# Sixteen subtractions of weight halves on VectorE instead of GpSimd, and the conversion steps grouped at the head of a pair's step

## The chip, the cores and the metric

One core of a Trainium2 chip runs the whole kernel. The metric is the device time of one execution in microseconds (us); lower is better. Times are medians over several runs.

## The reference

Two parts follow each other. The attention part takes `q`, `k`, `v` of 4 batches, 8 heads, 576 positions and 64 features. It computes causal softmax attention, and mixes it head by head with a linear memory read-out:

```
scores = causal(q @ k.T / 8);  a = softmax(scores);  local = a @ v
q_p = elu(q) + 1
mem_out = (q_p @ M_prev) / (q_p . z_prev + 1e-6)
x = sigmoid(beta) * mem_out + (1 - sigmoid(beta)) * local
```

The second part takes the 2304 rows of `x`, each of 512 features, through four weight matrices that are given in float64 and used as float32:

```
out = ((x @ w1) * (x @ w2)) @ w3 @ w_out      # 512->1024, 1024->1024, 1024->512
```

## The kernel before

**Pairs.** The attention runs over 16 pairs of heads, four to a batch (`pair_step(p, F)`). A pair's work is cut into named pieces: transposes of the softmax rows (`t1`, `t2`, `th`, `t3a` and so on, line 236), the memory path of the next pair (`ma`, `mb`, `mc`, lines 138 to 159), the transposes of its result (`mt`, line 165), the products with `v` and `M_prev` (`mm`, `pv`, lines 273 to 283), the copy of the result into two parts `xs` (`fin`, lines 294 and 295: ScalarE writes the high part, VectorE the low part and with that frees the PSUM tile `x`), then the next pair's scores (`ss`, line 205 into `s` and into `sx`, which uses the PSUM space that `fin` frees), their masked row minima (`s_red`, line 182 on VectorE), exponentials (`e0` to `e4`, line 217 on ScalarE) and normalisation (`n2` to `n4`, lines 221 to 226 on VectorE).

**Filler.** The string `ORDER` lists the pieces of one pair. At every `F` the TensorE gets some matmuls of another job: during the first batch `w_gen`, which forms the product `w3 @ w_out` (line 429, then `wH` on ScalarE, line 434, and `wL` on VectorE, line 421); from the second batch on `moe_gen`, the two products of the rows that the batch before gave (lines 479 and 499). There are 13 such slots to a pair.

**Conversion.** Weights arrive as float64, read as pairs of 32-bit words. `conv_stages` turns a piece of 128 x 512 into float32 in stages: a load (line 305), `scale` on ScalarE (line 316, output `wp`, `w3s` or `wo`), `join` with two VectorE instructions (lines 320 and 321), and for the first products' weights (pieces 24 to 39) a `split`: ScalarE rounds `wp` into the high part in `wsp` (line 328), GpSimd subtracts it and writes the low part (line 329). A piece's buffer `wp` comes free for another `scale` once line 329 has run. The letter `c` in `ORDER` is one step of this pipeline (two from the second batch on): it splits piece k-2, joins piece k-1, asks for loads up to k+1 and scales piece k. `tick_ok` refuses a step while the product `w3 @ w_out` is not far enough (pieces 12 to 23), and refuses pieces from 32 on during the first batch; a filler that needs a piece asks for it itself with `conv_upto`.

**Who sets the order.** The program order gives priorities. A list scheduler lays out each engine's queue when the program is built: an engine takes the highest priority among what is ready by the scheduler's own clock, and `tc.high_priority` raises a few instructions. On the chip each queue then runs in that fixed order, and an instruction that waits holds all that stand behind it on its engine.

Of the kernel before, what the change touches and what calls it, by code (L numbers as in the profile page):

```python
# [13 lines left out]
ALU = mybir.AluOpType  # L14
# [4 lines left out]


ORDER = (
    "lv mt t1 c F "
    "lqn t2 th c F "
    "t3a t3b c F "
    "t4a c F "
    "t4b t5 c F "
    "mm pv ma c F "
    "fin F "
    "ss lq mb F "
    "F "  # L30
# [7 lines left out]
def f32(ap):  # L38
    return ap.bitcast(F32)
# [3 lines left out]
def attention_moe_kernel(  # L43
# [13 lines left out]
    nc = tc.nc  # L57
# [240 lines left out]
    def conv_stages(k, src, dh, dl):  # L298
        n = 512
        box = {}  # L300

        def load():
            t = x_p.tile([128, 2 * S], F32, tag=f"x{4 + k % 3}", name="wst")
            box["raw"] = t[:, 0:2 * n].bitcast(U32).rearrange("p (n w) -> p n w", w=2)
            nc.sync.dma_start(out=t[:, 0:2 * n].bitcast(U32), in_=src.bitcast(U32))

        def scale():
            if k < 24:
                box["raw"] = raws[src[0]][:, src[1]]
            if k < 24:  # L310
                box["p"] = dh()
            elif k < 36 and k % 4 > 1:
                box["p"] = big.tile([128, n], F32, tag=f"r{4 + k % 4}", name="wp")
            else:
                box["p"] = o_p.tile([128, n], F32, tag="o", name="wp")
            nc.scalar.activation(out=box["p"], in_=f32(box["raw"][:, :, 1]), func=ACTF.Prelu, scale=2.0 ** -111, alpha=-(2.0 ** 32))

        def join():
            p = box["p"].bitcast(U32)
            nc.vector.tensor_scalar(out=p, in0=p, scalar1=3, scalar2=None, op0=ALU.logical_shift_left)  # L320
            nc.vector.scalar_tensor_tensor(  # L321
                out=p, in0=box["raw"][:, :, 0], scalar=29, in1=p, op0=ALU.logical_shift_right, op1=ALU.bitwise_or
            )

        def split():
            if k < 24:
                return
            nc.scalar.activation(out=dh(), in_=box["p"], func=ACTF.Copy)
            nc.gpsimd.tensor_tensor(out=dl(), in0=box["p"], in1=f32(dh()), op=ALU.subtract)  # L329

        return load, scale, join, split

# [84 lines left out]
    def w_gen():  # L417
        box = {}

        def low(i):  # L420
            nc.vector.scalar_tensor_tensor(  # L421
                out=wL[i], in0=box.pop(i), scalar=2.0 ** -16, in1=f32(wH[i]), op0=ALU.mult, op1=ALU.subtract
            )

        def mm(ps, i, kc):
            conv_upto(max(wo_job[kc], w3_job[i][kc // 4]))
            w = big_t["w3", i]
            wo = big_t["wo", kc // 2]
            nc.tensor.matmul(ps, lhsT=w[:, 128 * kc:128 * kc + 128], rhs=wo[:, 512 * (kc % 2):512 * (kc % 2) + 512], start=(kc == 0), stop=(kc == 7))  # L429

        def high(i, ps):
            w_done[0] += 1
            with tc.high_priority(100):
                nc.scalar.activation(out=wH[i], in_=ps, func=ACTF.Copy, scale=2.0 ** -16)
            box[i] = ps

        first = [ps_m.tile([128, DM], F32, tag="m", name="m") for _ in range(2)]
        for kc in range(8):
            for i in range(2):
                mm(first[i], i, kc)  # L440
                if kc == 7:
                    high(i, first[i])
                yield 870
        low(0)
        for i in range(2, NF):
            ps = ps_m.tile([128, DM], F32, tag="m", name="m")
            for kc in range(8):
                mm(ps, i, kc)
                yield 870
                if kc == 0:  # L450
                    low(i - 1)
            high(i, ps)
        low(NF - 1)
# [55 lines left out]
    def moe_gen(b):  # L509
        for n in (2 * b, 2 * b + 1):  # L510
            yield from gemm1(n)
            while 128 * (done_g[0] + 1) <= U * (n + 1):
                yield from gemm2(done_g[0])
                done_g[0] += 1
# [34 lines left out]
    def pair_step(p, F):  # L549
# [46 lines left out]
        out=mask[:, 448:576], in_=mask[:, 448:576], pattern=[[-1, 128]], compare_op=ALU.is_ge,  # L596
# [14 lines left out]
    F = Fill(w_gen(), W_NS, SLOTS * NC + PRE, wait=-4)  # L611
# [38 lines left out]
    for b in range(B):  # L650
        load_m(b)
        if b:
            limit[0] = NJ + 2
            F = Fill(moe_gen(b - 1), MOE_NS, SLOTS * NC)
# [3 lines left out]
    F = Fill(moe_gen(B - 1), MOE_NS, 1)  # L658
# [34 lines left out]
```

## Time and profile before

| | us |
|---|---|
| median of 3 runs | 572.43 (571.6 to 573.46) |
| the profiled execution, its own time | 571.37 |
| its span, first to last instruction | 569.6 |
| outside the span (571.37 - 569.6) | 1.77 |

The span is the time between the first and the last instruction of the profiled execution, which runs 1.77 us longer than its span and 1.06 us shorter than the median. Busy time is the time in which an engine had an instruction in execution, waits not counted.

### The profile page before, as it was taken

The numbers are of one execution on the slowest core, as the hardware profiler recorded it, in microseconds if no ns is written. First come the engines' busy times: TensorE is split into PE (matmuls) and PEld (weight loads), VectorE is DVE, ScalarE is ACT, GpSimd is POOL, SyncE is SP. The second block draws the span as 40 slices with busy tenths as digits, with TensorE's granted clock in tenths as the row PEclk, the third lists the DMA queues.
The fourth block names the chain that finished last, engine by engine and source line by source line (L and its number), as shares of the span: only waits on it lengthen the run. The fifth ranks groups of instructions, "written<-read, shape, count | busy, mean of one in ns | idle before, by whom it ended". The sixth has DMA issues, their size and how long they took to land.

```text
span 569.6 us, 9266 instructions
## 1 busy us (share of the span) xinstructions
PE 545.4 (96%) x3440; PEld 436.4 (77%) x3440; DVE 279.4 (49%) x880; ACT 277.5 (49%) x723; POOL 126.6 (22%) x153
## 2 busy tenths in 40 slices
PE   4899897899999999999999999999999999999997
PEld 2344554456797889788988898797969797998995
DVE  6986797838662626263726272724535351111111
ACT  5565785648562546454644455444635362130210
POOL 1101333015613032303230313021310320130220
PEclk9899989799999999999999999999999999999999
DMA  7991653713021312130202121322012000001001
GB/s 292 421 379 49 223 181 121 223 48 102 31 68 29 105 29 67 34 109 29 66 20 92 29 68 34 91 64 68 26 36 99 23 1 6 33 1 38 1 1 55
DMA packets 23069, 48.31 MB, mean 85 GB/s; under 512 B 6896, under 2 KB 13040, under 8 KB 21488
## 3 DMA queue, kind: packets, MB, share of 16 engines
q1 hardware_dynamic: 23024, 47.72, 25.1%
q8 instruction: 27, 0.44, 0.3%
q14 instruction: 18, 0.15, 0.1%
HBM read 43.00 MB, written 4.72 MB: 84 GB/s over the span
## 4 chain that ended last, share of the span: by engine, by line
PE 82%; DVE 8%; ACT 4%; issue 2%; POOL 2%; DMA 2%; SPq 0%; POOLq 0%; DVEq 0%
PE m L479 36%; PE m L499 18%; PE x L283 7%; PE s L236 7%; PE s L205 4%; PE m L429 4%; PE x L274 2%; PE sx L205 2%; DVE sm L226 2%; PE x L165 1%; DVE sm L182 1%; POOL wsp L329 1%; DMA wst<-w_out 1%; ACT pt L267 1%; PE s L191 1%
## 5 line engine op out<-in xcount | busy, mean ns | idle before, releaser
L479 PE MATMUL m<-xs,wsp 128*128 128x288 f32 x1536 | 221.6, 299 | 1.3 <-DVE wL L421 1.3
L479 PEld LDWEIGHTS m<-xs,wsp 128*128 128x128 f32 x1536 | 206.7, 188 | 2.3 <-DVE wL L421 1.5
L491 POOL TENSOR_TENSOR ht<-a,ht 128x288 fp32r<-128x288 f32 (+2 forms) x96 | 57.6, 612 | 237.5 <-ACT ht L490 237.5
L217 ACT ACTIVATE sm<-sm,mx 128x320 f32<-128x320 f32 (+2 forms) x144 | 82.7, 576 | 39.5 <-DVE mx L182 38.5
L499 PE MATMUL m<-wH,ht 128*128 128x512 f32 x288 | 94.2, 396 | 0.0
L488 DVE SCALAR_TENSOR_TENSOR a<-m,a 128x288 f32<-128x288 f32 x64 | 29.1, 455 | 99.1 <-PE m L479 94.7
L267 ACT ACTIVATE pt<-s 128x512 f32<-128x512 f32 (+1 forms) x144 | 63.3, 492 | 25.1 <-PE s L236 25.0
L429 PE MATMUL m<-wo,w3s 128*128 128x512 f32 x128 | 65.5, 647 | 6.2 <-DVE w3s L321 3.8
L499 PEld LDWEIGHTS m<-wH,ht 128*128 128x128 f32 x288 | 54.1, 188 | 11.2
L490 ACT ACTIVATE ht<-a 128x288 fp32r<-128x288 f32 (+2 forms) x96 | 31.5, 360 | 63.2 <-DVE a L488 63.1
L236 PE MATMUL s<-ident,sm 128*128 128x128 f32 x448 | 61.7, 273 | 0.0
L236 PEld LDWEIGHTS s<-ident,sm 128*128 128x128 f32 x448 | 52.7, 140 | 7.2 <-issue 5.8
L226 DVE TENSOR_SCALAR sm<-sm,sums 128x320 f32<-128x320 f32 (+2 forms) x144 | 57.1, 457 | 0.4
L182 DVE CUSTOM_DVE_ANT_0 sm<-s,mask 128x320 f32<-128x320 f32 (+3 forms) x112 | 44.4, 448 | 24.4 <-PE s L205 24.3
L499 PE MATMUL m<-wL,ht 128*128 128x512 f32 x144 | 56.2, 390 | 0.0
L146 POOL TENSOR_TENSOR e<-qn,z 128x640 f32<-128x640 f32 x16 | 25.3, 1581 | 136.3 <-DVE qn L144 112.9
L485 ACT ACTIVATE a<-m 128x288 f32<-128x288 f32 x64 | 26.1, 408 | 50.7 <-PE m L479 45.4
L429 PEld LDWEIGHTS m<-wo,w3s 128*128 128x128 f32 x128 | 24.4, 209 | 31.3 <-issue 20.0
L283 PEld LDWEIGHTS x<-pt,v 128*64 128x64 f32 x384 | 25.1, 137 | 29.9 <-issue 24.0
L283 PE MATMUL x<-pt,v 128*64 128x448 f32 (+4 forms) x384 | 46.7, 393 | 0.0
L295 DVE TENSOR_TENSOR xs<-x,xs 128x576 fp32r<-128x576 f32 x16 | 12.1, 756 | 66.6 <-ACT xs L294 66.6
L205 PE MATMUL s<-raw 64*128 64x320 f32 (+3 forms) x256 | 38.3, 414 | 4.5 <-DMA raw<-qkt 4.5
(65 smaller groups left out, 474.3 us busy)
## 6 DMA issues: line engine op xcount, KB each, us to landing
raw<-qkt SPq DMA_DIRECT2D x16, 576.0 KB, 3.9
wst<-w3t SPq DMA_DIRECT2D x8, 1024.0 KB, 8.9
wst<-w SPq DMA_DIRECT2D x16, 512.0 KB, 3.8
qn<-qn SPq DMA_DIRECT2D x16, 320.0 KB, 3.0
v<-v SPq DMA_DIRECT2D x32, 160.0 KB, 2.3
out<-o SPq DMA_DIRECT2D x18, 256.0 KB, 2.0
wst<-w_out SPq DMA_DIRECT2D x4, 1024.0 KB, 12.0
z<-z_prev SPq DMA_DIRECT2D x16, 64.0 KB, 2.9
```

The source lines that it names most:

```text
L182: nc.vector.tensor_tensor_reduce(out=sm[a][c][:, lo:hi] if c else sm0[:, 0:64], in0=x, in1=mask[:, S - KE[c] + lo:S - KE[c] + hi] if c els ...
L205: nc.tensor.matmul(y, lhsT=t[r, 0, 128 * c - 64:128 * c + 64], rhs=t[r, 1, lo:hi], start=True, stop=True)
L217: nc.scalar.activation(out=x, in_=x, func=ACTF.Exp, bias=mx, scale=-1.0, accum_out=sums_of(p)[:, k:k + 1])
L226: nc.vector.tensor_scalar(out=x, in0=x, scalar1=sums_of(p)[:, k:k + 1], scalar2=None, op0=ALU.mult)
L236: tr = lambda o, c, a, kc: nc.tensor.transpose(ps[:, o:o + 128], sm[a][c][:, 128 * kc:128 * kc + 128], ident)
L267: nc.scalar.activation(out=d, in_=s, func=ACTF.Copy)
L283: nc.tensor.matmul(x[64 * a:64 * a + 64, 384 + q0:384 + q1], lhsT=vv[:, a, kc], rhs=pt[:, a, o:o + q1 - q0], start=False, stop=(q0 == 0 or ...
L429: nc.tensor.matmul(ps, lhsT=w[:, 128 * kc:128 * kc + 128], rhs=wo[:, 512 * (kc % 2):512 * (kc % 2) + 512], start=(kc == 0), stop=(kc == 7))
L479: nc.tensor.matmul(ps[:, 0:U], lhsT=w[:, i, x, j], rhs=x_t[NC * b + j][:, xx, U * u:U * u + U], start=(k == 0), stop=(k == 11))
L490: nc.scalar.activation(out=hbuf(f, 0)[:, p:p + c], in_=a[:, o:o + c], func=ACTF.Copy)
L491: nc.gpsimd.tensor_tensor(out=hbuf(f, 1)[:, p:p + c], in0=a[:, o:o + c], in1=f32(hbuf(f, 0)[:, p:p + c]), op=ALU.subtract)
L499: nc.tensor.matmul(ps, lhsT=hbuf(f, a)[:, p:p + 128], rhs=b[f], start=(k == 0), stop=(k == 23))
```

## The change

Two edits. The subtraction at the end of `split` is issued on VectorE where it was issued on GpSimd: sixteen instructions of 128 x 512, with the same operands. And in `ORDER` the six letters `c`, which stood one each before the first six slots of a pair, stand two, two, one and one before its first four slots.

```
 ORDER = (
-    "lv mt t1 c F "
-    "lqn t2 th c F "
+    "lv mt t1 c c F "
+    "lqn t2 th c c F "
     "t3a t3b c F "
     "t4a c F "
-    "t4b t5 c F "
-    "mm pv ma c F "
+    "t4b t5 F "
+    "mm pv ma F "
     "fin F "
...
             nc.scalar.activation(out=dh(), in_=box["p"], func=ACTF.Copy)
-            nc.gpsimd.tensor_tensor(out=dl(), in0=box["p"], in1=f32(dh()), op=ALU.subtract)
+            nc.vector.tensor_tensor(out=dl(), in0=box["p"], in1=f32(dh()), op=ALU.subtract)
```

## Rows read from the trace of the kernel before

**Rows 1.** The page: busy us of each engine, share of the span, instructions.

```profile
PE 545.4 (96%) x3440; PEld 436.4 (77%) x3440; DVE 279.4 (49%) x880; ACT 277.5 (49%) x723; POOL 126.6 (22%) x153
```

**Rows 2.** Busy time by stretch: length, engines, PE clock, DMA; pairs 1 to 3, the rest.

```profile
60.00:81.10 21.10, 18.70 (x98) 11.14 (x99) 18.15 (x60) 17.34 (x43) 8.54 (x8) 0.92 0.62 200
81.10:110.90 29.80, 24.98 (x111) 13.52 (x110) 25.37 (x58) 18.65 (x43) 7.81 (x6) 0.89 0.51 163
110.90:133.10 22.20, 22.20 (x112) 12.47 (x111) 13.25 (x49) 13.45 (x35) 4.25 (x4) 1.00 0.31 90
...
162.00:569.60 407.60, 403.93 (x2749) 351.87 (x2747) 152.90 (x514) 172.73 (x472) 81.94 (x112) 1.00 0.14 45
```

**Rows 3.** The instructions of line 329 by stretch: length, POOL busy (count), PE clock, DMA.

```profile
60.00:81.10 21.10, 5.68 (x5) 0.92 0.62 200
110.90:133.10 22.20, 1.45 (x2) 1.00 0.31 90
60.00:150.00 90.00, 22.25 (x16) 0.94 0.42 133
```

**Rows 4.** Waits of PE from 60 to 150 us: total us, times, longest.

```profile
PE sx L205 <- DVE xs L295: 5.5, 2, 3.2
PE s L191 <- DVE mx L182: 1.6, 1, 1.6
PE m L479 <- DVE wL L421: 1.3, 1, 1.3
```

**Rows 5.** Timeline of PE: start, us, instruction.

```profile
73.58 7.68 PE L429 MATMUL m<-wo,w3s 128*128 128x512 f32 x14
...
104.21 6.86 PE L429 MATMUL m<-wo,w3s 128*128 128x512 f32 x12
...
127.88 5.37 PE L429 MATMUL m<-wo,w3s 128*128 128x512 f32 x12
```

**Rows 6.** Timeline of DVE in pair 2: start, us, instruction, idle before it.

```profile
88.93 1.68 DVE L320 TENSOR_SCALAR wp<-wp 128x512 uint32<-128x512 uint32 x1 [0.22 <-ACT wp L316]
...
97.53 1.04 DVE L320 TENSOR_SCALAR wp<-wp 128x512 uint32<-128x512 uint32 x1 [1.25 <-ACT wp L316]
...
99.21 0.75 DVE L295 TENSOR_TENSOR xs<-x,xs 128x576 fp32r<-128x576 f32 x1
...
100.33 1.63 DVE L321 SCALAR_TENSOR_TENSOR wp<-wst,wp 128x512 uint32<-128x512 uint32 x1
```

**Rows 7.** Timeline of POOL in the same stretch.

```profile
88.79 1.54 POOL L146 TENSOR_TENSOR e<-qn,z 128x640 f32<-128x640 f32 x1 [6.60 <-DVE qn L144]
...
97.02 1.26 POOL L329 TENSOR_TENSOR wsp<-wp,wsp 128x512 fp32r<-128x512 f32 x1 [1.75 <-ACT wsp L328]
100.04 1.38 POOL L329 TENSOR_TENSOR wsp<-wp,wsp 128x512 fp32r<-128x512 f32 x1 [1.75 <-ACT wsp L328]
```

**Rows 8.** Groups of instructions, whole run: count, busy us, mean ns, idle before.

```profile
L329 POOL TENSOR_TENSOR wsp<-wp,wsp 128x512 fp32r<-128x512 f32 x16 | 22.3, 1395 | 29.6 <-ACT wsp L328 29.5
...
L321 DVE SCALAR_TENSOR_TENSOR wp<-wst,wp 128x512 uint32<-128x512 uint32 x16 | 14.3, 892 | 0.4
...
L320 DVE TENSOR_SCALAR wp<-wp 128x512 uint32<-128x512 uint32 x16 | 10.3, 641 | 5.1 <-ACT wp L316 5.1
...
L328 ACT ACTIVATE wsp<-wp 128x512 fp32r<-128x512 f32 x16 | 10.1, 637 | 7.6 <-DVE wp L321 7.6
...
L320 DVE TENSOR_SCALAR w3s<-w3s 128x512 uint32<-128x512 uint32 x16 | 6.7, 420 | 1.6 <-ACT w3s L316 1.5
...
L421 DVE SCALAR_TENSOR_TENSOR wL<-m,wH 128x512 fp32r<-128x512 f32 x8 | 5.5, 683 | 3.2 <-ACT wH L434 3.2
```

**Rows 9.** Waits of ACT from 60 to 150 us.

```profile
ACT wp L316 <- POOL wsp L329: 3.8, 4, 1.5
```

**Rows 10.** Timeline of DVE, the normalisations of two successive pairs.

```profile
110.36 2.02 DVE L226 TENSOR_SCALAR sm<-sm,sums 128x320 f32<-128x320 f32 x7
...
130.84 4.09 DVE L226 TENSOR_SCALAR sm<-sm,sums 128x320 f32<-128x320 f32 x7
```

## Prediction

> **What bounds the kernel now.** I first read the page's busy line: TensorE (PE) is busy 545.4 of 569.6 us, 96% [rows 1]. Then I cut the span by pairs, each stretch beginning where PE takes up the five transposes of line 165. From 162 us to the end PE is busy 403.93 of 407.60 us at full granted clock [rows 2]; no conversion runs there, so the change has nothing to move. All sixteen of its subtractions lie between 60 and 150 us [rows 3]. In that part pair 3 is the nearly clean case: 22.20 us, PE busy throughout, granted clock 1.00, and 1.45 us of line 329 at its very end [rows 2, 3]. Pair 2 does the same PE work (111 records against 112) in 29.80 us, 7.60 longer, at a mean clock of 0.89 [rows 2]. So the question is what holds PE in pairs 1 and 2 and at the start of the second batch.
>
> The third view, PE's waits, names three places [rows 4]: `sx` waits for `fin`'s low part (line 295, VectorE, called DVE) 5.5 us in two waits, the score of block 0 waits for the row minima (line 182, DVE) 1.6 us, and the first batch product waits for `wL` (line 421, DVE) 1.3 us. All three releasers are DVE. A slow clock comes on top: twelve matmuls of line 429 take 5.37 us at clock 1.00 and 6.86 us behind the waits of pair 2; fourteen take 7.68 us behind the wait of pair 1 (5.5 - 3.2 = 2.3 us) [rows 4, 5], where 14/12 of 5.37 would be 6.27. The slow clock thus costs about 1.5 us in pair 2 and 1.4 in pair 1.
>
> The last view says why DVE is late: the timelines of DVE and GpSimd (POOL) side by side. Line 320 takes 0.420 us on `w3s` (mean of 16), but 1.68 us when it starts 0.14 us behind a POOL instruction of 1.54 us, and 1.04 us inside POOL's line 329; line 321 takes 1.63 us beside another line 329 and ends 0.54 us after it [rows 6 to 8]. In these rows a DVE instruction that meets a POOL one runs only when that has ended.
>
> **What the change removes.** Sixteen instructions leave POOL, 22.3 us in all, 1.395 each [rows 8]. POOL is busy for 126.6 us of the span, so its own time is worth nothing; what counts is whom it holds. The conversion's DVE instructions show that by group: line 320 averages 0.641 us on `wp` against 0.420 on `w3s`, line 321 averages 0.892 against 0.683 for line 421, the nearest unhindered form of that size [rows 8]. That is 16 x 0.221 + 16 x 0.209 = 6.9 us, part of it owed to POOL's other lines 146 and 159, which stay. Seven normalisations take 4.09 us at 130.84 against 2.02 one pair before: 2.1 more [rows 10]. Also ScalarE (ACT) waits 3.8 us in four waits for line 329 to free `wp` [rows 9].
>
> **What it adds.** Sixteen DVE subtractions of 128 x 512. None is in the trace; the nearest row, line 421, has the same size and takes 0.683 us. So 16 x 0.683 = 10.9 us of DVE work, against some 9.0 us of hindrance (6.9 + 2.1), of which lines 146 and 159 keep a part. DVE's total hardly falls. The gain, if any, is in position: the release of `wp` comes 1.395 - 0.683 = 0.7 us sooner per piece, and instructions on the path are no longer held.
>
> One page speaks against the edit: the Trainium skill, "SBUF — State Buffer", section "Who interferes with whom", says that a DVE instruction with two SBUF inputs contends with a GpSimd instruction that reads SBUF, and that the second to start fully blocks. The trace agrees where it can: line 321 has two such inputs and took 1.63 us beside POOL's 1.38 [rows 6, 7]. By it the moved subtraction can itself be held by lines 146 and 159, each time by up to 1.54 us; if four of the sixteen met them in full, the gain below of 3.1 us would shrink to nothing.
>
> **Pair 2.** The chain in front of `sx` is: line 320 at 97.53 (held 1.04 - 0.42 = 0.62 us), line 321, line 295 at 99.21; behind it line 321 at 100.33 (held 1.63 - 0.68 = 0.95 us), in front of the row minima [rows 6]. Taking line 329 off POOL removes 1.57 us there. Two pieces release 0.7 us earlier each: 1.4. Two subtractions now stand in DVE's queue at these places: +1.4 (2 x 0.683). Net -1.6 us of waiting, of 4.8 in this pair (3.2 + 1.6). A third of the 1.5 us of slow clock should go with it: -0.5. I take -1.9, rounding down. Ends: the whole excess over pair 3, -7.6, and +1.4 if the subtractions come in front and nothing else moves.
>
> **Pair 1.** Its 2.3 us wait is also for line 295. Which instruction holds DVE there the rows above do not say, and POOL also runs lines 146 and 159 in this pair. I take 0. Ends: -3.7 (the wait and its 1.4 us of slow clock) and +0.7 (one subtraction in front of line 295).
>
> **Start of the second batch.** Line 421 stands behind the normalisations that lost 2.1 us; PE waits 1.3 us for it [rows 4, 10]. Line 421 is older in program order than the subtractions beside it, so these should fall behind it. I take -1.2. The other end is 0, where two subtractions (1.4 us) go ahead.
>
> **The moved steps.** From the code's counts: in pair 0 pieces 16 and 17 are now refused, since the filler has not ended its first product by slots 3 and 4, and go to pair 1; pieces 18 to 31 stay in their pairs, earlier by up to two slots; pieces 36 to 39 move from slots 3 and 4 of pair 4 to slot 2. Each step takes its load, `scale`, `join` and `split` along, and the loads pass that of `qn` on the DMA queue, which is asked for a whole pair ahead of its transposes. I cost this at nothing. The pieces do not run at their place now: five of the subtractions already run in pair 1 [rows 3], though their steps belong to pair 2 and later. Readiness of a load and of a `wp` buffer decides, and priority only settles ties. If that cover is gone, the price is one `scale` and one `split` of ACT ahead of a `pt` copy: about 1.3 us (2 x 0.637) in pair 4.
>
> **Sum.** -1.9 + 0 - 1.2 + 0 = -3.1 us. Against the profiled execution's own 571.37: 568.3. That execution was 1.06 us under the median of the runs, so the median becomes 569.3, 0.55% less.
>
> **Rivals.** (a) *Clean pair.* Without POOL's holds, `fin` and the minima come in time, and pair 2 runs like pair 3: -7.6, with -1.3 for the batch start: 571.37 - 8.9 + 1.06 = 563.5. For it: pair 3 shows that the PE work fits 22.2 us. Against: DVE is busy 25.37 us in pair 2 [rows 2], which holds the hindrance but would also hold the new work.
>
> (b) *The lock only changes sides.* The subtraction is held by lines 146 and 159, or stands where the hindrance stood; 10.9 us in, 9.0 out. No change: 571 to 573.5. For it: the two totals are near, and lines 146 and 159 remain.
>
> (c) *DVE's queue waits for ACT.* This is the slower side. On POOL a subtraction waited 29.6 us in total for line 328 and held nothing that mattered [rows 8]. On DVE it holds all behind it. If each of some eight subtractions between 60 and 110 us arrives one line 328 (0.637 us) early, DVE stands 5.1 us, on top of 8 x 0.683 = 5.5 of work; about half of the 9.0 us of hindrance goes, 4.5. That is +6.1 us on DVE in two pairs where it releases every PE wait; with -1.2 at the batch start +4.9: 577.3. It decides once 3 of the eight are held with DVE followed by PE: 3 x 0.637 + 5.5 - 4.5 - 1.2 = +1.7 us. For it: ACT already waits 7.6 us for DVE in front of line 328 [rows 8], so queue orders and real times disagree there. Against: DVE has idle time in these pairs too (2.95 and 4.43 us).
>
> **Numbers.** Forecast 0.45 (of it 0.03 within 0.3%), (a) 0.12, (b) 0.20, (c) 0.23. Within 0.3% (1.7 us) is what a measurement of this kernel cannot tell from no change. Faster 0.42 + 0.12 = 0.54; same 0.23; slower 0.23. The range goes from (a), 563.5, to just below the far end of (c), which needs all eight held: 576.5. The forecast's own range is 566.5 to 571.5.
>
> **What would show it.** Right: no DVE instruction beside a missing line 329 is held; line 320 on `wp` falls towards 0.42 us mean; subtractions at 0.68 us; the waits of `sx` for line 295 fall from 5.5 to about 4; the wait for line 421 is gone; nothing changes behind 162 us but the start. Wrong: DVE idle in front of line 329 with line 328 as the releaser, pair 2 still near 29.8 us, a clock below 0.9 in pairs 1 or 2, or a new PE wait in pair 4 for `pt`. The queue order is laid out anew, so a piece that lands ahead of line 295 can move the sum by the size of a whole wait.

## The result and the profile after

The changed kernel takes 567.19 us (median of 4 runs, 566.53 to 568.34) against 572.5 for the kernel before (4 runs): a ratio of 0.9909 with a 95% interval of 0.9886 to 0.9933, 0.9% faster. A second series gave 568.14 us, ratio 0.9926 [0.9908, 0.9945]. The forecast was 569.3, 0.55% faster. The profiled execution took 566.9 us, 4.5 less than the one before, with a span of 565.1.

The page's busy line, to set against [rows 1]. POOL has 16 instructions and 20.5 us less; DVE has 16 instructions more and yet 1.2 us less busy time.

```profile
PE 544.0 (96%) x3440; PEld 435.1 (77%) x3440; DVE 278.2 (49%) x896; ACT 277.0 (49%) x723; POOL 106.1 (19%) x137
```

Busy time by stretch, cut where PE takes up line 165, as in [rows 2]: pairs 1, 2 and 3. Both tables begin at 60.00, a little after pair 1 does.

```profile
60.00:79.10 19.10, 16.93 (x97) 9.88 (x96) 16.18 (x50) 15.48 (x39) 3.27 (x2) 1.00 0.61 202
79.10:107.30 28.20, 24.43 (x112) 12.91 (x111) 24.86 (x73) 20.53 (x49) 3.21 (x2) 0.94 0.52 171
107.30:129.50 22.20, 22.20 (x112) 12.47 (x111) 13.81 (x50) 13.58 (x35) 2.80 (x2) 1.00 0.36 115
```

The waits of PE from 60 to 150 us, to set against [rows 4]. The wait of `sx` is nearly halved, that for line 421 is gone, that for the row minima has grown, and a new one of 0.5 us for line 226 stands in pair 2.

```profile
PE sx L205 <- DVE xs L295: 2.9, 2, 1.9
PE s L191 <- DVE mx L182: 2.3, 1, 2.3
PE s L236 <- DVE sm L226: 0.5, 1, 0.5
PE s L236 <- ACT pt L267: 0.3, 1, 0.3
```

PE's queue holds the same instructions in the same order in both kernels, so the two timelines can be laid on each other. Pair 1 begins at 59.62 (60.08 before), pair 2 at 79.08 (81.10), pair 3 at 107.30 (110.91), pair 4 at 129.46 (133.08); the products with `M_prev` of pair 4 (line 274) begin at 141.16 in the chain of work, where they began at 146.33. The differences give the gain by place: 0.5 us before pair 1, 1.6 in pair 1, 1.6 in pair 2, nothing in pair 3, 1.55 at the start of the second batch, 5.2 in all. By the end 0.7 us of it has gone again, some 0.4 of it behind the last matmul (565.54 before, 560.63 after) and the rest in small pieces for which no wait stands out.

PE's timeline at the places of [rows 5], first a line of the kernel before in pair 2, then the kernel after. In pair 1 the same fourteen matmuls of line 429 now take 6.23 us. In pair 2 the wait for `fin` shrinks to 1.00 us and the four matmuls of `sx` behind it from 1.76 to 1.13; the next wait grows to 2.30, and the twelve matmuls behind it are as slow as before.

```profile
100.02 1.76 PE L205 MATMUL sx<-raw 64*128 64x512 f32 x4 [3.19 <-DVE xs L295]
```

```profile
71.52 1.13 PE L205 MATMUL sx<-raw 64*128 64x512 f32 x4 [1.86 <-DVE xs L295]
...
73.02 6.23 PE L429 MATMUL m<-wo,w3s 128*128 128x512 f32 x14
...
96.53 1.13 PE L205 MATMUL sx<-raw 64*128 64x512 f32 x4 [1.00 <-DVE xs L295]
...
100.12 0.43 PE L191 MATMUL s<-raw,qd 128*128 128x64 f32 x2 [2.30 <-DVE mx L182]
100.39 7.07 PE L429 MATMUL m<-wo,w3s 128*128 128x512 f32 x12
```

Groups of instructions over the whole run, as in [rows 8]. Lines 320 and 321 on `wp` fell from 0.641 and 0.892 us to 0.483 and 0.687; the moved subtraction takes 0.809.

```profile
L329 DVE TENSOR_TENSOR wsp<-wp,wsp 128x512 fp32r<-128x512 f32 x16 | 12.8, 809 | 3.4 <-ACT wsp L328 3.4
...
L321 DVE SCALAR_TENSOR_TENSOR wp<-wst,wp 128x512 uint32<-128x512 uint32 x16 | 10.9, 687 | 0.2
...
L320 DVE TENSOR_SCALAR wp<-wp 128x512 uint32<-128x512 uint32 x16 | 7.6, 483 | 0.7 <-ACT wp L316 0.5
```

Rows of DVE's timeline. At the batch start the seven normalisations of [rows 10] are back at 2.03 us. In pair 1 one subtraction takes 2.03 us, since POOL's line 146 runs from 67.87 to 69.53. In pair 2 two subtractions stand between line 295 (95.73) and the row minima.

```profile
68.04 2.03 DVE L329 TENSOR_TENSOR wsp<-wp,wsp 128x512 fp32r<-128x512 f32 x1
...
96.39 1.28 DVE L329 TENSOR_TENSOR wsp<-wp,wsp 128x512 fp32r<-128x512 f32 x2
...
127.93 2.03 DVE L226 TENSOR_SCALAR sm<-sm,sums 128x320 f32<-128x320 f32 x7
```

```profile
67.87 1.66 POOL L146 TENSOR_TENSOR e<-qn,z 128x640 f32<-128x640 f32 x1 [8.30 <-DVE qn L144]
```

The same place in the kernel before, DVE first, then POOL. The instruction that stood in front of line 295 there, line 321 at 68.51, was held by the same line 146; line 329 held line 144 ahead of it, 1.33 us against 0.83 after.

```profile
66.81 1.33 DVE L144 SCALAR_TENSOR_TENSOR qn<-qn,e 128x640 f32<-128x640 f32 x1 [2.88 <-ACT e L139]
...
68.51 1.91 DVE L321 SCALAR_TENSOR_TENSOR wp<-wst,wp 128x512 uint32<-128x512 uint32 x1
```

```profile
66.18 1.28 POOL L329 TENSOR_TENSOR wsp<-wp,wsp 128x512 fp32r<-128x512 f32 x1 [6.15 <-ACT wsp L328]
68.22 1.65 POOL L146 TENSOR_TENSOR e<-qn,z 128x640 f32<-128x640 f32 x1 [0.76 <-DVE qn L144]
```

Besides the holds, the release of `wp` shows. VectorE's waits for `scale` (line 316) from 60 to 150 us fell from 5.1 to 0.5 us (first row before, second after), and ScalarE's wait for line 329 to free `wp` from 3.8 [rows 9] to 2.3 (third row).

```profile
DVE wp L320 <- ACT wp L316: 5.1, 7, 1.8
```

```profile
DVE wp L320 <- ACT wp L316: 0.5, 1, 0.5
```

```profile
ACT wp L316 <- DVE wsp L329: 2.3, 2, 1.6
```

### The profile page after: what moved, and what is told of

Read it like the earlier page. It is cut to its first block, busy times and chain, and to the rows that moved or that the text cites. A ratio compares the mean times of both kernels' runs of the same rounds, so it can differ in the third digit from the quotient of the medians.

```text
span 565.1 us, 9261 instructions
## 1 busy us (share of the span) xinstructions
PE 544.0 (96%) x3440; PEld 435.1 (77%) x3440; DVE 278.2 (49%) x896; ACT 277.0 (49%) x723; POOL 106.1 (19%) x137
## 3 DMA queue, kind: packets, MB, share of 16 engines
HBM read 43.00 MB, written 4.72 MB: 84 GB/s over the span
## 4 chain that ended last, share of the span: by engine, by line
PE 86%; DVE 8%; ACT 2%; DMA 2%; issue 1%; POOL 1%; SPq 0%; DVEq 0%; POOLq 0%
PE m L479 36%; PE m L499 18%; PE s L236 7%; PE x L283 7%; PE s L205 5%; PE m L429 5%; PE sx L205 2%; PE x L274 2%; PE x L165 1%; DVE sm L182 1%; DMA wst<-w 1%; PE s L191 1%; DVE sm L226 1%; DVE w3s L321 1%; DVE wp L321 1%
## 5 line engine op out<-in xcount | busy, mean ns | idle before, releaser
L499 PEld LDWEIGHTS m<-wH,ht 128*128 128x128 f32 x288 | 54.1, 188 | 11.3
L146 POOL TENSOR_TENSOR e<-qn,z 128x640 f32<-128x640 f32 x16 | 26.1, 1632 | 152.2 <-DVE qn L144 152.2
L226 DVE TENSOR_SCALAR sm<-sm,sums 128x320 f32<-128x320 f32 (+2 forms) x144 | 54.0, 436 | 0.3
```

The source lines that it names most:

```text
L226: nc.vector.tensor_scalar(out=x, in0=x, scalar1=sums_of(p)[:, k:k + 1], scalar2=None, op0=ALU.mult)
L499: nc.tensor.matmul(ps, lhsT=hbuf(f, a)[:, p:p + 128], rhs=b[f], start=(k == 0), stop=(k == 23))
```

## The experiments

Two theories stood against each other. The first: line 329 on GpSimd costs the time, by holding VectorE's instructions or by freeing `wp` late, and taking it away gives the time back. The second: what counts is the new order of the queues that the regrouped letters `c` bring. Beside them stood two doubts of the prediction: that VectorE's own added work, or its waiting for ScalarE, eats the gain. Ratios are against the kernel before on the same chip.

**e1: the subtraction on VectorE alone.**

```
-            nc.gpsimd.tensor_tensor(out=dl(), in0=box["p"], ...)   # in the kernel before
+            nc.vector.tensor_tensor(out=dl(), in0=box["p"], ...)
```

> The subtraction on VectorE, the letters c left as in the kernel before. If the gain of 5.3 us comes from taking line 329 off GpSimd (its holds on VectorE, the later release of wp), most of it is here: 567 to 569 us, no VectorE instruction held by line 329, the PE wait for line 421 at the batch start gone. If the gain comes from the regrouped steps, this kernel stays at 571.5 to 573.5.

568.04 us, ratio 0.9924 [0.9907, 0.9942]: the same as the whole change within its interval. The wait for line 421 at the batch start is gone.

**e2: the regrouped letters alone.** `ORDER` as after, line 329 on `nc.gpsimd`.

> The regrouped letters c, the subtraction left on GpSimd. If line 329 on GpSimd is the cause, 571 to 573 us with pair 2 near 29 us and lines 320 and 321 on wp still well above 0.42 and 0.68 us on average. If the regrouping is the cause, 567 to 569. Pieces 16 and 17 are refused in pair 0 in this kernel too, so the 0.46 us that pair 0 gave should be here.

572.01 us, ratio 1.000 [0.999, 1.001]. PE's waits are those of [rows 4]:

```profile
PE sx L205 <- DVE xs L295: 5.7, 2, 3.3
PE m L479 <- DVE wL L421: 1.3, 1, 1.3
PE s L191 <- DVE mx L182: 1.1, 1, 1.1
```

Pair 1 starts at 59.65 us here and at 59.99 in e1 (60.08 before), so the 0.4 us of pair 0 belongs to the regrouping; in the time it does not show. The gain comes with the subtraction and not with the letters: the first theory stands, the second falls. By which of its two ways the subtraction gains, e3 and e8 ask.

**e3: the hold put back without the rest.** Behind each subtraction on VectorE, one instruction on GpSimd that multiplies the low part by one.

```
             nc.vector.tensor_tensor(out=dl(), in0=box["p"], in1=f32(dh()), op=ALU.subtract)
+            nc.gpsimd.tensor_tensor(out=dl(), in0=f32(dl()), in1=one.to_broadcast([128, 512]), op=ALU.mult)
```

> The kernel after, with one more GpSimd instruction behind each split that multiplies the low part just written by one: 16 instructions of 128x512 that read SBUF on GpSimd, no buffer wp waits for them, and VectorE still does the subtraction. The values stay the same. If the holds are what GpSimd's line 329 cost, VectorE's lines 320, 321, 226 beside them stretch again and the time rises by 2 to 6 us, to 569 to 573, above all in pair 2 and at the batch start. If the gain came from the earlier release of wp (a shorter chain), nothing is lost: 567 to 568.

574.06 us, ratio 1.0031 [1.0021, 1.004]: some 6 to 7 us above the kernel after, above the expected range and above the kernel before too. No `wp` waits for these instructions, and VectorE hardly waits for `scale` (0.1 us in front of line 320 on `wp`, 5.1 in the kernel before). So the earlier release of `wp`, which this kernel keeps, is not enough for the gain; what share of it the release has no run shows. The groups on `wp` are stretched again, as before the change (0.892 and 0.641 there):

```profile
L321 DVE SCALAR_TENSOR_TENSOR wp<-wst,wp 128x512 uint32<-128x512 uint32 x16 | 14.5, 911 | 0.2
...
L320 DVE TENSOR_SCALAR wp<-wp 128x512 uint32<-128x512 uint32 x16 | 10.5, 659 | 0.1
```

Pair 2 takes 32.0 us. In it, DVE's two instructions in front of the row minima meet two such multiplications, which run from 100.66 to 103.26 us (first block DVE, second POOL):

```profile
101.33 1.04 DVE L320 TENSOR_SCALAR wp<-wp 128x512 uint32<-128x512 uint32 x1
102.40 1.41 DVE L321 SCALAR_TENSOR_TENSOR wp<-wst,wp 128x512 uint32<-128x512 uint32 x1
```

```profile
100.66 2.60 POOL L329 TENSOR_TENSOR wsp<-wsp,one 128x512 fp32r<-128x512 f32 x2 [2.83 <-DVE wsp L329]
```

Not all of the 6 us need be a hold of VectorE. In pair 1 a multiplication also keeps GpSimd's own line 146 waiting behind it, 0.9 us after the line 144 that it needs (68.31 to 69.17), and line 146 then holds the subtraction in front of line 295 (2.02 us at 69.41). The shares were not taken apart.

**e8: the same extra instruction on VectorE.** The counterpart of e3, with `nc.vector` for `nc.gpsimd` in the added line.

> The kernel after, with the same extra multiplication by one as in the run that put it on GpSimd, here on VectorE: 16 more VectorE instructions of 128x512. On GpSimd it cost 6.9 us over the kernel after. If what it cost there was GpSimd's hold on VectorE, the same instruction in VectorE's own queue costs less, 1 to 4 us (its 0.69 us each where VectorE is late, in pairs 1 and 2): 568 to 571. If VectorE's amount of work is what bounds these pairs, it costs at least as much here: 573 or more.

568.54 us, ratio 0.994 [0.9921, 0.9958], against 0.9926 for the kernel after in the same series: 0.4 us more by the medians, 0.8 by the ratios, whose intervals overlap, for 11.3 us of VectorE work.

```profile
L329 DVE TENSOR_TENSOR wsp<-wsp,one 128x512 fp32r<-128x512 f32 x16 | 11.3, 715 | 0.0
```

One and the same instruction costs 6 to 7 us on the engine with time to spare and less than 1 us on the busy one. VectorE's amount of work is not the limit at this size; what an instruction on GpSimd holds up is.

**e10 and e11: eight pieces each.** The subtraction on VectorE for pieces 24 to 31 only, or for 32 to 39 only.

```
+            (nc.vector if k < 32 else nc.gpsimd).tensor_tensor(out=dl(), ...)    # e10
+            (nc.vector if k >= 32 else nc.gpsimd).tensor_tensor(out=dl(), ...)   # e11
```

> The kernel after, with the subtractions of pieces 32 to 39 back on GpSimd; those of 24 to 31 stay on VectorE. If the gain is the sum of places (profiles: 0.5 us in pair 0, 1.6 in pair 1, 1.6 in pair 2, 1.6 at the start of the second batch), this keeps some 3.6 us of it: 568.5 to 570, and PE's wait of 1.3 us for line 421 at the batch start is back. If one place holds all of it, this is 567.5 to 568.5 or 571.5 to 572.5.

> The kernel after, with the subtractions of pieces 24 to 31 back on GpSimd; those of 32 to 39 stay on VectorE. If the gain is the sum of places, this keeps 1.6 us at the batch start and the 0.5 of pair 0: 570 to 571, pairs 1 and 2 as in the kernel before, no wait for line 421. If one place holds all of it, 567.5 to 568.5 or 571.5 to 572.5.

e10: 569.83 us, ratio 0.9955 [0.9938, 0.9973]. e11: 570.26 us, ratio 0.9966 [0.9954, 0.9979]. Both lie in the ranges expected for a sum of places. The two gains, 0.45 and 0.34%, add up to 0.79%, near the whole. In e10 the wait for line 421 is back; in e11 it is gone and pair 2 keeps its long wait:

```profile
133.78 1.87 PE L479 MATMUL m<-xs,wsp 128*128 128x288 f32 x12 [1.28 <-DVE wL L421]
```

```profile
99.86 1.94 PE L205 MATMUL sx<-raw 64*128 64x512 f32 x4 [3.38 <-DVE xs L295]
```

**e6 and e7: what stands in front of the row minima in pair 2.** Pieces 32 to 35 (e6) or only 34 and 35 (e7) get their buffers `wp` from space that w3 pieces hold until late in the first batch.

```
-            elif k < 36 and k % 4 > 1:
-                box["p"] = big.tile([128, n], F32, tag=f"r{4 + k % 4}", name="wp")
+            elif 24 <= k < 36 and (k > 31 or k % 4 > 1):        # e7: and k % 4 > 1
+                box["p"] = (ring if k > 31 else big).tile([128, n], F32,
+                    tag=f"g{k % 4}" if k > 31 else f"r{4 + k % 4}", name="wp")
```

> The kernel after, with the buffers wp of pieces 32 to 35 in space that the w3 pieces hold until late in the first batch, so that these four pieces, which only the second batch needs, can't be scaled and joined in pair 2. If they are what stands ahead of line 295 and of the row minima there, pair 2 falls from 28.2 us by 2 to 4 and the kernel to 563 to 565.5 us. If the pair is bound by other work of VectorE, or the four pieces are late in the second batch, 567 to 569.

569.67 us, ratio 0.9964 [0.995, 0.9978]: slower than the kernel after and above both ranges expected. Pair 2 did fall by 3.0 us, but pair 3 rose from 22.2 to 28.9:

```profile
78.90:104.10 25.20, 22.73 (x112) 12.31 (x111) 23.28 (x69) 19.01 (x46) 3.21 (x2) 1.00 0.53 169
104.10:133.00 28.90, 24.98 (x111) 13.57 (x110) 18.48 (x58) 16.51 (x40) 2.80 (x2) 0.88 0.36 107
```

There DVE stood 4.72 us at a line 320 whose load had come late, the row minima waited behind it, PE idled 3.92 us, and its next twelve matmuls took 7.93 us (one row each of DVE and ACT, then two of PE):

```profile
123.19 0.43 DVE L320 TENSOR_SCALAR wp<-wp 128x512 uint32<-128x512 uint32 x1 [4.72 <-ACT wp L316]
```

```profile
122.50 0.66 ACT L316 ACTIVATE wp<-wst 128x512 f32<-128x512 f32 x1 [5.71 <-DMA wst<-w]
```

```profile
124.77 0.69 PE L191 MATMUL s<-raw,qd 128*128 128x64 f32 x2 [3.92 <-DVE mx L182]
125.25 7.93 PE L429 MATMUL m<-wo,w3s 128*128 128x512 f32 x12
```

> The kernel after, with only pieces 34 and 35 kept out of pair 2 (their buffers wp in space that w3 pieces 6 and 7 hold). With all four out, pair 2 fell by 3.0 us but VectorE's queue stood 4.7 us in pair 3 in front of a line 320 whose load was late. If two pieces fit in pair 3's idle time without such a stand, half of pair 2's gain stays: 565 to 566.5. If any late piece makes the queue stand again, 567.5 to 570.

567.13 us, ratio 0.9917 [0.9894, 0.994] against 0.9926 [0.9908, 0.9945] for the kernel after: not to be told from it, and between the two ranges expected. In its profile the wait for the minima fell to 1.0 us, and PE got a new wait of 1.37 us for line 226 in pair 3.

**e4: no GpSimd at all beside the conversion.** Lines 146 and 159 of pairs 1 to 4 on VectorE.

```
-        nc.gpsimd.tensor_tensor(out=e, in0=t, in1=zb, op=ALU.mult)
+        (nc.vector if 1 <= p <= 4 else nc.gpsimd).tensor_tensor(out=e, in0=t, in1=zb, op=ALU.mult)
...
-        nc.gpsimd.tensor_tensor(out=tv, in0=tv, ...)
+        (nc.vector if 1 <= p <= 4 else nc.gpsimd).tensor_tensor(out=tv, in0=tv, ...)
```

> The kernel after, with lines 146 and 159 of pairs 1 to 4 on VectorE too, so that GpSimd runs nothing beside the conversion until the second batch's own work. If the two lines' remaining holds (one subtraction 2.03 us, two line 320s 1.82) still cost the path, 563 to 566 us. If the added VectorE work (8 instructions of 128x640, some 0.8 us each) costs as much as the holds, 566.5 to 568.5.

567.0 us, ratio 0.9896 [0.9871, 0.9922]; the intervals overlap, so by itself this is unclear. Line 320 on `wp` is down to 0.419 us and the subtraction to 0.724. In pair 1, with line 146 off GpSimd, the wait for `fin` is 0.67 us, where it was 1.86.

**e9: e4 and e7 together.**

> The kernel after with both of the variants that came out no slower: lines 146 and 159 of pairs 1 to 4 on VectorE, and pieces 34 and 35 kept out of pair 2. If their effects are separate, 564.5 to 566.5 us. If VectorE is now the limit in these pairs, or the late pieces make its queue stand in pair 3, 566.5 to 568.5.

563.96 us, ratio 0.9852 [0.9836, 0.9869]: 1.5% faster than the kernel before and, by intervals that do not meet, faster than the kernel after, and below the range expected. POOL is idle in pairs 1 to 3; the two long waits of `sx` are one of 0.7 us; pair 2 takes 26.4 us. (This profiled execution took 566.35 us, the slowest of the kernel's runs; it starts pair 1 2.2 us later than e4.)

```profile
62.10:80.70 18.60, 16.50 (x95) 9.69 (x94) 16.65 (x56) 15.99 (x39) 0.00 (x0) 1.00 0.49 163
80.70:107.10 26.40, 24.20 (x110) 13.06 (x111) 24.16 (x70) 19.01 (x46) 0.00 (x0) 0.94 0.59 191
```

## Why the prediction was right, step by step

**The bound and the cause.** Right. PE follows VectorE in pairs 1 and 2 and at the batch start, and line 329 on GpSimd made VectorE late: e1 and e2 show that the gain comes with it, e3 and e8 that an instruction on GpSimd costs what the same one on VectorE does not, e10 and e11 that both halves of the pieces count. Two limits stay. In pair 1 line 329 was the smaller part: line 144 lost 0.5 us to it, and line 321 lost 1.2 us (1.91 against 0.69) to line 146, which stays. The wait there fell by 0.5 us in the first profile of the kernel after and not at all in the second (2.37). And how the gain divides between the holds and the earlier release of `wp` is argued from the traces, not shown by a run.

**Pair 2: -1.9 forecast, -1.6 measured.** Right in size, though not in its parts, so the nearness is in part luck: the wait for `fin` lost 2.2 us, more than the 1.6 forecast for both waits, the wait for the minima gained 0.7, and a new wait for line 226 took 0.5. Of the slow clock a part did go, as forecast, but at another place: the four matmuls of `sx` took 0.63 us less, while the twelve of line 429 took 7.07 us instead of 6.86; the granted clock of the pair rose from 0.89 to 0.94.

**Pair 1: 0 forecast, -1.6 measured.** This is the term that was mis-sized. The wait fell only from 2.3 to 1.9 us. What came back was the slow stretch behind it: the granted clock stayed at 1.00, and the fourteen matmuls took 6.23 us instead of 7.68, 1.45 us less. That price stood in the prediction as the far end and was given no share of the value. It does not follow from the length of the wait alone. How often it comes back is not shown; the mean clock of the runs suggests most of them (last section).

**Batch start: -1.2 forecast, -1.55 measured.** Right in size and in the cause: line 421 no longer has held normalisations in front of it. Not right in the order: two subtractions do go ahead of it (127.32 and 129.94), which the prediction had as the case without a gain, and the last two normalisations, which stood in front of it, now stand behind (131.20). It starts 1.2 us after pair 4 does, where it started 4.0 after, and PE does not wait for it.

**The moved steps: 0 forecast.** Right within what the runs can tell (e2: 1.000; e1 against the whole change). The 0.4 us of pair 0 that they bring in the profile was not foreseen.

**VectorE's added work.** It was priced at 1.4 us in pair 2, and there two subtractions of 1.28 us do stand in front of the row minima, and PE's wait for these grew by 0.7. Elsewhere it cost little: e8 doubles it everywhere for 0.4 to 0.8 us. The 1.4 us set against it for the earlier release of `wp` no run measures by itself. Rival (c) did not decide either: VectorE did wait for line 328, 3.4 us in two waits, but 2.8 of them in a stretch in which it had nothing that PE waited for.

**Rival (b), and the rule on the second SBUF input.** The Trainium skill's "SBUF — State Buffer", section "Who interferes with whom", holds here: the subtraction of 68.04 was blocked by line 146 until that had ended. The subtractions average 0.809 us, 16 x (0.809 - 0.683) = 2.0 us in all, nearly all of it in two of them: 2.03 us at 68.04 and 1.30 at 141.92. The first takes the place of line 321, which line 146 held before, so it is no new loss in pair 1. The prediction wanted four full meetings to use up its 3.1 us; 2 x 1.54 us make that already.

**Rival (a), the clean pair.** Not reached: pair 2 still takes 28.2 us. e6 shows a part of what is left: lines 320 and 321 of a piece that only the second batch needs stand between line 295 and the minima. The wait for `fin` stays at 1.00 us there, the wait for the minima falls to 1.00, and the twelve matmuls take 5.37. In the profiles pair 2 takes 25.5 us in e7, 26.1 in e4 and 26.4 in e9, so what e9 gains over either alone can't be read from this pair. The 4 us that e9 has left over pair 3 are mostly the 2.1 us wait for the minima and slow matmuls behind it. In its trace one subtraction, two line 320s, a wait of 1.11 us for `scale` and one line 321 stand between line 295 and the minima; taking them away was not tried.

## What to carry to other kernels

An idle engine is not a free place for work. Before moving an instruction, compare the durations of its neighbours' instructions, form by form, where the two engines run side by side and where they do not; the excess (9.0 us here) says what there is to win on the neighbour. How much of it reaches the time (4.5 us in the profiles) hangs on what TensorE waits for. And an instruction doubled once on either engine says which of the two is the limit. A wait of TensorE can have a second price, the slow matmuls that may follow it: give it a share of the sum. And since each queue runs in a fixed order, delaying work by making its buffer late can move the wait to whatever stands behind it, as in e6.

## What the runs showed of the hardware

A wait of PE can be followed by a slow stretch. In pair 1 of the kernel before, PE waits 2.32 us, and from 73.4 to 76.0 us the granted clock is 0.50, the lower of its two levels (1.2 GHz of 2.4); in the kernel after it is 1.00 from 73 to 79 us, behind a wait of 1.86. But the stretch does not follow from the wait's length alone. In eleven profiles the wait for `fin` in pair 1 is followed by the same fourteen matmuls of line 429. In the five with a wait under 2 us (1.83 to 1.86) these took 6.23 us. Of the six with 2.1 to 2.7 us, four were slow and two were not: 7.74 us behind 2.12 (e8), 7.68 behind 2.32 (before), 7.92 behind 2.35 (e2) and 7.68 behind 2.48 (e11), but 6.23 behind 2.37 (the kernel after, second series) and 6.23 behind 2.68 (e3):

```profile
72.88 1.13 PE L205 MATMUL sx<-raw 64*128 64x512 f32 x4 [2.68 <-DVE xs L295]
...
74.38 6.23 PE L429 MATMUL m<-wo,w3s 128*128 128x512 f32 x14
```

Such a stretch is worth about 1.5 us. What decides it was not found. The same kernel can have the wait at 1.86 us in one execution and at 2.37 in another. The mean granted clock over a whole run goes with the spread of the times: the ten runs of e10 are five of 567.75 to 569.53 us at a clock of 0.990 and five of 570.14 to 572.22 at 0.984 to 0.987. It goes with the change too: of the kernel before, 55 of 59 runs beside the experiments have 0.985 or less, of the kernel after 9 of 10 have 0.988 or more. In which stretch the runs without a kept trace lost their clock is not shown.

A small VectorE instruction was held as long as a large one. In the kernel before, line 152 on 128 x 10 elements took 1.28 us beside a line 329 that ran from 92.09 for 1.27 us; in the kernel after, with no GpSimd instruction beside it, 0.17.
